# Attention, MLP and capacity routing on one core: the product with v turned round, sums beside it, maxima placed by a mask

## The chip, the cores and the metric

The kernel runs on one core of one Trainium2 chip. The core has a matrix engine (PE, whose weight loads the profile lists apart as PEld), a vector engine (DVE), a scalar engine (ACT), GpSimd (POOL) and a sync engine (SP), whose queue issues nearly all transfers here. Each engine works through its own instructions in order and waits on semaphores. The metric is the device time of one execution in microseconds. In the profile a tile's name is the name given in the code, without buffer numbers.

## The reference

Three stages follow each other: attention with normalised q and k, an MLP with a gated activation, and a mixture of experts with a fixed capacity.

```python
batch, n_heads, seq, head_dim = (4, 12, 448, 64)

def _attn_ref(q, k, v, g_q, g_k):
    def rmsnorm(x, g):
        rms = np.sqrt(np.mean(x * x, axis=-1, keepdims=True) + 1e-06)
        return x / rms * g
    q_n, k_n = (rmsnorm(q, g_q), rmsnorm(k, g_k))
    scale = 1.0 / np.sqrt(q.shape[-1])
    scores = scale * np.matmul(q_n, k_n.transpose(0, 1, 3, 2))
    scores = scores - np.max(scores, axis=-1, keepdims=True)
    attn = np.exp(scores)
    attn = attn / (np.sum(attn, axis=-1, keepdims=True) + 1e-09)
    return np.matmul(attn, v).astype(np.float32)

def _moe_ref(x, w_in, w_out):          # x: 1792 tokens of 768
    h = x @ w_in                       # 768 x 2048
    relu6 = np.clip(h + 3.0, 0.0, 6.0)
    g = h * relu6 / 6.0
    return (g @ w_out).astype(np.float32)
```

The third stage (`_moe2_ref`) gives each of 1792 tokens to one of 8 experts by its logits, at most 224 tokens to each, and runs two products with a ReLU between them per expert. The weights `w_in` and `w_out` arrive as 64-bit floats; everything else is 32-bit.

## The kernel before

The 48 heads are worked on in 24 pairs `i`, six pairs to a batch. The two heads of a pair (`s` = 0, 1) stand in the two halves of the 128 partitions where the contraction runs over the 64 values of a head, and a head's 448 positions are cut into four blocks `c` of 112 (`CP`). Precision is held by splitting: a float32 value becomes a rounded part (`...h`) and a remainder (`...l`) in the type float32r, and a product becomes three.

The steps of a pair, with the names that the profile shows:

- `load` (L208): q, k and v of the pair into `ld_q`, `ld_k`, `ld_v`, 224 KB each.
- `sums`, `invert` (L224, L242): squares on ACT, their sums on DVE, inverse roots on DVE. For the first three pairs the squares read `ld_q` and `ld_k`; for all others, which are done in groups of three or six, q and k are loaded a second time, into `sq` (L237). There are seven groups.
- `norm` (L251): POOL multiplies (`xn`). `transp` (L290): four transposes each for q and k on PE, then ACT writes the rounded part (`qh`, `kh`) and DVE the remainder (`ql`, `kl`).
- `s1` (L313): a first product q k in one rounded part, queries in partitions, from which DVE takes the maxima `mx`. `mt` (L326): PE transposes the maxima, ACT copies them negated (`mrow`), and two small transfers put them as a row into `mr`.
- `sT` (L338): the full scores `st`, keys in partitions, with the row of maxima added by a product with `onerow`; ACT takes the exponentials `ph`.
- `av` (L363): the product with v. The weights (the stationary side) are `va`, 112 keys by 128 columns, 64 of them v and 64 of them ones; the moving side is `ph`, 448 queries wide, in plain float32. So the numerators of a head stand in 64 partitions of `av` and copies of the sums in the other 64.
- `fin`, `fin_r`, `fin_x` (L381 to L415): ACT copies the sums (`sm`) and numerators (`num`), a transfer turns the row of sums into columns (`scol`), DVE takes the reciprocals, a transfer writes them to memory (`r_dr`), another reads them back spread over 64 partitions per head (`rc`), POOL multiplies, ACT writes the rounded part `xh`, POOL the remainder `xl`.

`xh` and `xl` of a batch are the input of the MLP's first product (`h`, L447), 288 products a batch, in the order that `mlp1_atoms` gives. These and, late in the attention, the products that fold the gate's weights into `w_out` (`wprime_atoms`) stand in a list from which `fill` takes some between the steps of later pairs. `conv_in` and `conv_out` narrow the 64-bit weights meanwhile: each of 32 blocks is loaded into the one buffer `wraw`, taken apart by four DVE instructions (`cv`, L128 to L131) and written back.

The order on PE is written out by hand. Each step of a pair has a due time in a table, 16 units to a pair; events are sorted by it, and `fill` spreads the list of atoms between them. For ACT, DVE, POOL and SP the recording layer chooses the order from its own estimate. The table's lines that matter:

```python
T_LOAD, T_NORM, T_Q, T_K, T_V = -56, -38, -30, -29, -5
T_S1, T_MT = (-24, -20, -16, -12), -9.5
T_ST, T_AV, T_FIN = (0, 4, 8, 12), ((4.5, 8.5, 12.5, 14.5), (9, 13, 17, 20)), 2
T_R, T_X, T_MLP = 4, (6, 9, 12), 16
```

PSUM is one pool of eight banks for all of this. After the attention come the last batch's first product, the second product (`y`, L1039), the routing, and the experts.

Of the kernel before, what the change touches and what calls it, by code (L numbers as in the profile page):

```python
# [8 lines left out]
F32 = mybir.dt.float32  # L9
# [4 lines left out]
OP = mybir.AluOpType  # L14
# [7 lines left out]
def kernel(  # L22
# [31 lines left out]
    PB = 4  # L54
# [11 lines left out]
    FULL = B * H  # L66
# [12 lines left out]
    r_dr = [dram.tile([2, S], F32, name=f"r_dr{i}")[:] for i in range(B * NP)]  # L79
# [92 lines left out]
    onerow = const.tile([128, CP], F32R, name="onerow")  # L172
    nc.vector.memset(onerow.bitcast(F32), 0.0)
    eps = const.tile([128, 1], F32, name="eps")
    nc.vector.memset(eps, 1e-9)
    mrs = []
    for s in range(2):
        nc.vector.memset(onerow[64 * s:64 * s + 1, :].bitcast(F32), 1.0)
    for n in range(OB):
        mrs.append(apool.tile([128, S], F32R, name=f"mr{n}", bufs=1))  # L180
        nc.gpsimd.memset(mrs[n].bitcast(F32), 0.0)
    VS = {}

    def vtiles(i):

        f = full(2 * i)
        key = (f, i % 2)
        if key not in VS:
            va = apool.tile([CP, 2, NCH, 128], F32 if f else F32R, name="va", bufs=2)
            w = va if f else va.bitcast(F32)  # L190
            nc.gpsimd.memset(w[:, 0, :, 64:], 1.0)
            nc.gpsimd.memset(w[:, 1, :, :64], 1.0)
            vl = None
            if not f:
                vl = apool.tile([CP, NCH, 192], F32R, name="vl", bufs=2)
                nc.gpsimd.memset(vl[:, :, 64:128].bitcast(F32), 0.0)
            VS[key] = va, vl
        return VS[key]

# [4 lines left out]
    def full(h):  # L204

        return h < FULL

    def load(i):  # L208
        b, j = divmod(i, NP)
        ts = []  # L210
        for nm, src in (("q", q), ("k", k), ("v", v)):
            t = apool.tile([CP, 2, NCH, D], F32, name=f"ld_{nm}")
            nc.sync.dma_start(t.rearrange("p h c d -> p h (c d)"),
                              src[b, 2 * j:2 * j + 2].rearrange("h (p c) d -> p h (c d)", p=CP))
            ts.append(t)
        QKV[i] = ts
# [3 lines left out]
    GROUPS = [(0,), (1,), (2,), (3, 4, 5)] + [tuple(range(g, g + 6)) for g in range(6, NH2, 6)]  # L220
# [1014 lines left out]
```

## Time and profile before

| | us |
|---|---|
| median of 3 runs | 1428.04 |
| lowest, highest run | 1416.88, 1430.52 |
| the profiled execution | 1415.71 |
| its span, first to last instruction | 1413.9 |
| mean granted clock of PE | 0.941 |

In the profile's head each engine's busy time stands with its share of the span:

```profile
span 1413.9 us, 19042 instructions
PE 1219.4 (86%) x6704; PEld 934.2 (66%) x6704; DVE 762.0 (54%) x1517; ACT 589.8 (42%) x1115; POOL 436.9 (31%) x320
PE   1477688878788979977878999999999989999998
PEclk9987889998899999999999999999999999999999
```

The last two lines cut the span into 40 slices of 35 us; a digit is the busy share of PE, and below it the share of its clock that was granted, in tenths. A float32 product is two records on PE, so the 192 products with v are 384 of the 6704. The attention covers the first 754 us, which are the slices in which PE has gaps.

### The profile page before, as it was taken

How to read it: one execution, taken by the hardware profiler on the slowest of the kernel's cores; microseconds unless marked ns; L12 is line 12 of the kernel's file. 1: busy time of each engine (PE TensorE's matmuls, PEld its weight loads, DVE VectorE, ACT ScalarE, POOL GpSimd, SP SyncE). 2: the span in 40 equal slices, each digit the busy share in tenths (PEclk: the TensorE clock that was granted, in tenths of full speed). 3: DMA queues.
4: the chain of work that ended last, by engine and by line, in shares of the span. 5: the costliest groups of instructions: out<-in, count | busy, mean ns of one | idle time of the engine just before them, and what ended most of it. 6: DMA issues, size and time to landing. Idle time of an engine off the chain costs nothing.

```text
span 1413.9 us, 19042 instructions
## 1 busy us (share of the span) xinstructions
PE 1219.4 (86%) x6704; PEld 934.2 (66%) x6704; DVE 762.0 (54%) x1517; ACT 589.8 (42%) x1115; POOL 436.9 (31%) x320
## 2 busy tenths in 40 slices
PE   1477688878788979977878999999999989999998
PEld 1233345555555656655557778777777779999997
DVE  6775655655462323333225974666666657666550
ACT  3354544333344434544445753111111256666650
POOL 1211222212121221211113442222222457767641
PEclk9987889998899999999999999999999999999999
DMA  7776655665663333233238984222222488888741
GB/s 185 206 213 174 163 155 159 192 193 171 182 189 93 93 104 81 80 105 91 79 98 263 321 269 131 60 75 69 63 74 58 113 229 232 248 251 255 228 152 40
DMA packets 247232, 216.97 MB, mean 153 GB/s; under 512 B 32160, under 2 KB 226400, under 8 KB 247136
## 3 DMA queue, kind: packets, MB, share of 16 engines
q1 hardware_dynamic: 243808, 204.74, 50.4%
q0 software_dynamic: 3328, 11.01, 2.5%
q8 instruction: 53, 0.87, 0.3%
q14 instruction: 43, 0.35, 0.1%
HBM read 177.17 MB, written 38.36 MB: 152 GB/s over the span
## 4 chain that ended last, share of the span: by engine, by line
PE 48%; DMA 27%; DVE 12%; issue 5%; ACT 4%; POOL 2%; SPq 1%; POOLq 0%; DVEq 0%; ACTq 0%
PE y L1039 14%; DMA rc<-r_dr 9%; PE h L447 8%; PE y L1187 7%; PE av L370 6%; PE h L1123 4%; DMA r_dr<-rcol 4%; DMA wraw<-in_moe_w_in_dram 3%; DMA wraw<-in_moe_w_out_dram 2%; DMA scol<-sm 2%; PE h L1125 2%; DMA sq<-in_q_dram 2%; PE st L345 2%; DMA win_v<-w 2%; DMA sq<-in_k_dram 2%
## 5 line engine op out<-in xcount | busy, mean ns | idle before, releaser
L370 PE MATMUL av<-ph,va 112*128 112x448 f32 x384 | 200.4, 651 | 33.1 <-DVE kl L307 15.6
L447 PE MATMUL h<-xh,wl 128*128 128x448 f32 x384 | 171.3, 446 | 0.0
L447 PE MATMUL h<-xh,wh 128*128 128x448 f32 x384 | 149.6, 389 | 9.3 <-ACT ph L354 5.9
L370 PEld LDWEIGHTS av<-ph,va 112*128 112x128 f32 x384 | 76.6, 219 | 110.1 <-issue 62.6
L447 PE MATMUL h<-xl,wh 128*128 128x448 f32 x384 | 148.9, 388 | 0.0
L983 POOL TENSOR_TENSOR g2l<-gr,g2h 128x512 fp32r<-128x512 f32 x60 | 78.6, 1311 | 202.0 <-ACT g2h L981 154.7
L106 POOL TENSOR_TENSOR wel<-we_s,weh 128x768 fp32r<-128x768 f32 x60 | 117.8, 1971 | 62.3 <-ACT weh L105 51.5
L105 ACT ACTIVATE weh<-we_s 128x768 fp32r<-128x768 f32 x128 | 105.7, 843 | 71.6 <-DMA we_s<-in_moe_w_dram 53.8
L106 DVE TENSOR_TENSOR wel<-we_s,weh 128x768 fp32r<-128x768 f32 x68 | 99.7, 1473 | 64.0 <-ACT weh L105 58.1
L1039 PE MATMUL y<-woh,g2l 128*128 128x512 f32 (+1 forms) x448 | 128.3, 348 | 1.0 <-POOL g2l L983 1.0
L322 DVE TENSOR_REDUCE mx<-s 112x1 f32<-112x448 f32 x192 | 110.4, 613 | 33.1 <-PE s L319 33.1
L1039 PE MATMUL y<-woh,g2h 128*128 128x512 f32 (+1 forms) x448 | 127.1, 347 | 0.0
L1039 PE MATMUL y<-wol,g2h 128*128 128x512 f32 (+1 forms) x448 | 126.0, 345 | 0.0
L981 ACT ACTIVATE g2h<-gr 128x512 fp32r<-128x512 f32 x60 | 37.7, 631 | 205.6 <-PE y L1039 157.5
L1123 PE MATMUL h<-xe,weh 128*128 128x448 f32 x384 | 121.2, 378 | 2.6 <-DVE xe L1074 2.6
L411 POOL TENSOR_TENSOR num<-num,rc 128x448 f32<-128x448 f32 x24 | 27.2, 1131 | 298.9 <-DMA rc<-r_dr 287.2
L354 ACT ACTIVATE ph<-st 112x448 f32<-112x448 f32 x192 | 93.0, 538 | 50.8 <-PE st L345 50.0
L106 POOL TENSOR_TENSOR wl<-win_v,wh 128x768 fp32r<-128x768 f32 x32 | 61.6, 1925 | 154.4 <-ACT wh L105 133.8
L447 PEld LDWEIGHTS h<-xh,wh 128*128 128x128 f32 x384 | 76.7, 200 | 29.5 <-issue 12.3
L447 PEld LDWEIGHTS h<-xh,wl 128*128 128x128 f32 x384 | 76.5, 199 | 25.2 <-issue 17.4
L1125 PE MATMUL h<-xe,wel 128*128 128x224 f32 x384 | 92.8, 269 | 0.0
L1187 PE MATMUL y<-weh,hl 128*112 128x384 f32 x256 | 86.5, 338 | 0.0
(235 smaller groups left out, 2496.2 us busy)
## 6 DMA issues: line engine op xcount, KB each, us to landing
we_s<-in_moe_w_dram SPq DMA_DIRECT2D x128, 384.0 KB
win_v<-w SPq DMA_DIRECT2D x64, 384.0 KB
g_dr<-g SPq DMA_DIRECT2D x64, 224.0 KB
gr<-g_dr SPq DMA_DIRECT2D x52, 256.0 KB
wraw<-in_moe_w_in_dram SPq DMA_DIRECT2D x16, 768.0 KB
wraw<-in_moe_w_out_dram SPq DMA_DIRECT2D x16, 768.0 KB
gr<-g_dr SPq DMA_DIRECT2D x48, 224.0 KB
w<-cv SPq DMA_DIRECT2D x16, 384.0 KB
```

What stands on the lines that cost most here:

```text
L105: nc.scalar.activation(hi, raw, AF.Copy)
L106: eng.tensor_tensor(lo, raw, hi.bitcast(F32), op=OP.subtract)
L322: mx = nc.vector.tensor_reduce(MX[i][:, s * NCH + c:s * NCH + c + 1], pp[s][:CP, :S], axis=AX.X, op=OP.max)
L354: nc.scalar.activation(e[:, s], pp[s][:CP, :S], AF.Exp)
L370: nc.tensor.matmul(p[:, :S], va[:, s, c, :], a, start=(c == 0), stop=(c == NCH - 1))
L447: nc.tensor.matmul(p[:, :S], w[:, c], x[:, c], start=(n == 0), stop=(n == 3 * NC - 1))
L981: nc.scalar.activation(gh, g, AF.Copy)
L983: eng.tensor_tensor(gl, g, gh.bitcast(F32), op=OP.subtract)
L1039: nc.tensor.matmul(pp[hf][:, :COLS[hf].stop - COLS[hf].start], a[:, f % QF], w[:, COLS[hf]], start=(f == 0 and n == 0), stop=(f == NF - 1 ...
L1123: mm = [lambda: nc.tensor.matmul(p[:, :4 * CP], wh[:, fo], x.rearrange("d k t -> d (k t)"), start=(c == 0), stop=(c == NC - 1), skip_group ...
L1125: lambda: nc.tensor.matmul(p[:, :2 * CP], wl[:, fo], x[:, 0], start=False, stop=False, skip_group_check=True)]
L1187: nc.tensor.matmul(p[:CP, :HW], a[:, f, tk], w[:, o], start=(f == 0 and n == 0), stop=(f == FB - 1 and n == 2))
```

## The change

The product with v changes sides. The exponentials, 112 keys by 112 queries, become the stationary side, and v with two columns of ones (66 columns, `vv`) the moving side. The queries then stand in the partitions, the numerators and the sums beside each other in one row. DVE adds 1e-9 to the sums (`scol`), copies the numerators (`num`), takes the reciprocals, POOL multiplies with them along the row (`xq`), PE turns the result back by four transposes (`xt`), ACT writes `xh` and DVE `xl`, both from PSUM. The transfers `scol`, `r_dr` and `rc` are gone.

The maxima are transposed as before, from a tile with a column for each block at 0 to 3 and 64 to 67, and DVE multiplies the result, repeated four times, with a mask (`place`) that keeps row `c` in block `c`; a product with -1 everywhere (`minus`) then sums over the partitions. `mrow` and its transfers are gone.

q and k are loaded once, each into three buffers; v is loaded by a step of its own, later. The squares are taken from these loads, in groups of one, one, and then two pairs (13 groups), through one buffer `sq` instead of two.

The due times are new. The product with v of a pair stands after all its scores, beside those of the next pair, one head after the other; the number of `ph` buffers goes from 4 (two heads each) to 12 (one head each).

The ACT queue in the second stage, where an MLP product runs beside the pairs, before the change:

```order
L354 ACTIVATE ph<-st 112x448 x2
L390 ACTIVATE sm<-av,eps 1x448
L392 ACTIVATE num<-av 64x448
L283 ACTIVATE va<-ld_v 112x4x64
L390 ACTIVATE sm<-av,eps 1x448
L392 ACTIVATE num<-av 64x448
L283 ACTIVATE va<-ld_v 112x4x64
L354 ACTIVATE ph<-st 112x448 x2
L105 ACTIVATE wh<-win_v 128x768
```

and a few rows on in the same pair:

```order
L354 ACTIVATE ph<-st 112x448 x2
L413 ACTIVATE xh<-num 128x448
L330 ACTIVATE mrow<-t 8x112
L105 ACTIVATE wh<-win_v 128x768
L450 ACTIVATE r<-h,half 128x448
L354 ACTIVATE ph<-st 112x448 x4
```

The same engine and place after the change:

```order
L319 ACTIVATE ph<-st 112x448 x2
L252 ACTIVATE vv_113<-ld_v 112x8x64
L107 ACTIVATE wh<-win_v 128x768
L417 ACTIVATE r<-h,half 128x448
L319 ACTIVATE ph<-st 112x448 x2
L381 ACTIVATE xh<-t 128x448
L107 ACTIVATE wh<-win_v 128x768
L417 ACTIVATE r<-h,half 128x448
L319 ACTIVATE ph<-st 112x448 x2
```

The copies of sums and numerators and the row of maxima have left ACT, and `xh` now reads PE's transposes (`t`) instead of POOL's `num`.

The DVE queue in the second stage after the change, where a block of `w_out` is converted (`cv`) beside a pair; `mr` are the placed maxima, and `scol` and `num` read the product with v:

```order
L130 TENSOR_SCALAR cv<-wraw 128x768
L419 SCALAR_TENSOR_TENSOR g<-r,h 128x448
L289 TENSOR_REDUCE mx_109<-s_1721 112x1
L289 TENSOR_REDUCE mx_109<-s_1722 112x1
L131 TENSOR_SCALAR cv<-cv 128x768
L297 TENSOR_TENSOR mr<-t,place 128x448
L363 TENSOR_SCALAR scol<-av,eps 112x4
L364 COPY num<-av 112x4x64
L132 SCALAR_TENSOR_TENSOR cv<-wraw,cv 128x768
L368 RECIPROCAL scol<-scol 112x8
```

Of these rows `mr`, `scol` and `num` are new on DVE, and they stand behind the first `cv`, which waits for a transfer.

The SP queue at the start of the program, the loads of the first pairs, before the change (`sq` is the second load of q and k):

```order
L213 DMA ld_q<-in_q_dram 112x2x256
L213 DMA ld_k<-in_k_dram 112x2x256
L213 DMA ld_v<-in_v_dram 112x2x256
L237 DMA sq<-in_q_dram 112x2x256
L237 DMA sq<-in_k_dram 112x2x256
L213 DMA ld_v<-in_v_dram 112x2x256
L556 DMA wg<-in_moe_w_gate_dram 128x6x8
L213 DMA ld_q<-in_q_dram 112x2x256
L213 DMA ld_k<-in_k_dram 112x2x256
```

and after it:

```order
L200 DMA ld_q<-in_q_dram 112x2x256
L200 DMA ld_k<-in_k_dram 112x2x256
L200 DMA ld_q<-in_q_dram 112x2x256
L200 DMA ld_k<-in_k_dram 112x2x256
L207 DMA ld_v<-in_v_dram 112x2x256 x2
L523 DMA wg<-in_moe_w_gate_dram 128x6x8
L207 DMA ld_v<-in_v_dram 112x2x256
L200 DMA ld_q<-in_q_dram 112x2x256
L200 DMA ld_k<-in_k_dram 112x2x256
```

Both pieces begin with the second pair's q and k; the third pair's stood seven rows on and now stand next.

The diff, cut to its core:

```diff
-    PB = 4
+    PB = 12
+    SQ = 1
+    SPLIT = False
-    T_LOAD, T_NORM, T_Q, T_K, T_V = -56, -38, -30, -29, -5
-    T_S1, T_MT = (-24, -20, -16, -12), -9.5
-    T_ST, T_AV, T_FIN = (0, 4, 8, 12), ((4.5, 8.5, 12.5, 14.5), (9, 13, 17, 20)), 2
-    T_R, T_X, T_MLP = 4, (6, 9, 12), 16
+    T_LOAD, T_VLOAD, T_NORM, T_Q, T_K, T_V = -72, -20, -38, -30, -28, 6
+    T_SUMS, T_INV = -50, -42
+    T_S1, T_MT = (-24, -20, -16, -12), -7
+    T_ST = (0, 4, 8, 12)
+    T_AV = ((17, 18, 19.5, 20.5), (22, 23, 24.5, 25.5))
+    T_NUM, T_XT, T_MLP = 28, 31, 35
...
+    place = const.tile([128, NCH, CP], F32, name="place")
+    nc.vector.tensor_tensor(place, ident[:, 0:NCH, None].to_broadcast([128, NCH, CP]),
+                            ident[:, 64:64 + NCH, None].to_broadcast([128, NCH, CP]), op=OP.add)
...
-    GROUPS = [(0,), (1,), (2,), (3, 4, 5)] + [tuple(range(g, g + 6)) for g in range(6, NH2, 6)]
+    GROUPS = [(0,), (1,)] + [(g, g + 1) for g in range(2, NH2, 2)]
...
-        for a, src in ((0, q), (1, k)):
-            sq = apool.tile([CP, 2 * NCH, D], F32, name="sq", bufs=2)
-            if len(g) == 1:
-                x = QKV[i][a]
-            else:
-                x = sq.rearrange("p (h c) d -> p h c d", h=2)
-                nc.sync.dma_start(x.rearrange("p h c d -> p h (c d)"),
-                                  src[b, 2 * j:2 * j + 2].rearrange("h (p c) d -> p h (c d)", p=CP))
-            nc.scalar.activation(sq, x.rearrange("p h c d -> p (h c) d"), AF.Square)
+        for a in range(2):
+            sq = apool.tile([CP, 2 * NCH, D], F32, name="sq", bufs=SQ)
+            nc.scalar.activation(sq, QKV[i][a].rearrange("p h c d -> p (h c) d"), AF.Square)
...
-        nc.tensor.transpose(t[:2 * NCH, :CP], MX[i], ident[:CP, :CP])
-        m = apool.tile([2 * NCH, CP], F32R, name="mrow")
-        nc.scalar.activation(m, t[:2 * NCH, :CP], AF.Copy, scale=-1.0)
-        MR[i] = mrs[i % OB]
-        for s in range(2):
-            nc.sync.dma_start(MR[i][64 * s:64 * s + 1].rearrange("a (c p) -> a c p", c=NCH).bitcast(F32),
-                              m[s * NCH:(s + 1) * NCH].bitcast(F32))
+        nc.tensor.transpose(t[:, :CP], MX[i].rearrange("p h c -> p (h c)"), ident[:CP, :CP])
+        MR[i] = apool.tile([128, NCH, CP], F32R, name="mr")
+        nc.vector.tensor_tensor(MR[i], t[:, None, :CP].to_broadcast([128, NCH, CP]), place, op=OP.mult)
...
-                nc.tensor.matmul(p[:, :S], va[:, s, c, :], a, start=(c == 0), stop=(c == NCH - 1))
+                nc.tensor.matmul(p[:CP, o:o + W], PP[i, s, c][0][:, qs], vv[:, s, c, 64:], start=(c == 0), stop=(c == NCH - 1))
...
+            nc.vector.tensor_scalar(sc[:, s, m], pv[:, :, 64], eps[:CP], None, op0=OP.add)
+            nc.vector.tensor_copy(num[:, m, s], pv[:, :, 0:64])
+
+    def normalize(i):
+        num, sc, xq = NUM[i]
+        nc.vector.reciprocal(sc, sc)
+        nc.gpsimd.tensor_tensor(xq, num, sc[:, :, :, None].rearrange("p h c o -> p c h o").to_broadcast([CP, NCH, 2, D]),
+                                op=OP.mult)
+
+    def xt(i):
...
+        for c in range(NCH):
+            nc.tensor.transpose(t[:, c * CP:(c + 1) * CP], xq[:, c].rearrange("p h d -> p (h d)"), ident[:CP, :CP])
+        nc.scalar.activation(xh[:, j], t[:, :S], AF.Copy)
+        nc.vector.tensor_tensor(xl[:, j], t[:, :S], xh[:, j].bitcast(F32), op=OP.subtract)
```

In the new `av` the loop runs over heads, blocks of queries `n` (`qs`) and blocks of keys `c`; `W` is 66, and four blocks of queries share one PSUM bank.

More of the change, by code (lines that the diff above doesn't have):

```diff
@@ L174 @@
     eps = const.tile([128, 1], F32, name="eps")
     nc.vector.memset(eps, 1e-9)
-    mrs = []
-    for s in range(2):
[L178 to L198, printed above, removed]
+    mxs = []
@@ L201 @@
+    for n in range(2):
+        mxs.append(apool.tile([CP, 2, 64], F32, name=f"mx{n}", bufs=1))
+        nc.gpsimd.memset(mxs[n], 0.0)
+    VW = 130
+    vvs = []
+    for n in range(2):
+        vvs.append(apool.tile([CP, 2, NCH, VW], F32R if SPLIT else F32, name=f"vv{n}", bufs=1))
+        nc.gpsimd.memset((vvs[n].bitcast(F32) if SPLIT else vvs[n])[:, :, :, 128:], 1.0)
     QKV, OPER, XT, FIRST, TR = {}, {}, {}, {}, {}
     NH2 = B * H // 2
-    def full(h):
-        return h < FULL
     def load(i):
@@ L395, in fin_r @@
-    def fin_r(i):
-        sc, num = SM[i]
-        rs = apool.tile([CP, 2, NCH], F32, name="rcol", bufs=2)
-        nc.vector.reciprocal(rs, sc)
-        nc.sync.dma_start(bass.AP(tensor=r_dr[i].tensor, offset=r_dr[i].offset, ap=[[NCH, CP], [S, 2], [1, NCH]]), rs)
-        rc = apool.tile([128, S], F32, name="rc", bufs=2)
-        nc.sync.dma_start(rc, bass.AP(tensor=r_dr[i].tensor, offset=r_dr[i].offset, ap=[[S, 2], [0, 64], [1, S]]))
-        SM[i] = (rc, num)
-    def fin_x(i, part):
+        for s in range(2):
+            if SPLIT:
+                e = apool.tile([CP, S], F32, name="pexp", bufs=2)
+                ph, pl = [apool.tile([CP, S], F32R, name=n, bufs=PB) for n in ("ph", "pl")]
+                nc.scalar.activation(e, pp[s][:CP, :S], AF.Exp)
+                nc.scalar.activation(ph, e, AF.Copy)
+                nc.gpsimd.tensor_tensor(pl, e, ph.bitcast(F32), op=OP.subtract)
+                PP[i, s, c] = (ph, pl)
+            else:
+                e = apool.tile([CP, S], F32, name="ph", bufs=PB)
+                nc.scalar.activation(e, pp[s][:CP, :S], AF.Exp)
+                PP[i, s, c] = (e,)
@@ L405, in fin_x @@
+    def normalize(i):
[4 more added lines that the diff above has]
+    def xt(i):
         b, j = divmod(i, NP)
-        rc, num = SM[i]
-        if i % NP == 0 and part == 0:
+        xq = NUM.pop(i)[2]
+        if j == 0:
             XT[b] = [xpools[b % 2].tile([128, NC, S], F32R, name=n) for n in ("xh", "xl")]
@@ L409, in fin_x @@
         xh, xl = XT[b]
-        if part == 0:
-            nc.gpsimd.tensor_tensor(num, num, rc, op=OP.mult)
-        elif part == 1:
-            nc.scalar.activation(xh[:, j], num, AF.Copy)
-        else:
-            nc.gpsimd.tensor_tensor(xl[:, j], num, xh[:, j].bitcast(F32), op=OP.subtract)
+        t = ps.tile([128, 512], F32, name="t", tag="b", bufs=8)
+        for c in range(NCH):
+            nc.tensor.transpose(t[:, c * CP:(c + 1) * CP], xq[:, c].rearrange("p h d -> p (h d)"), ident[:CP, :CP])
@@ L653 @@
         at(t + T_LOAD, load, i)
[L654 to L661 removed]
+        at(t + T_VLOAD, vload, i)
+        g = GROUP[i]
+        first = 16 * g[0]
+        at(first + T_SUMS + 4 * (i - g[0]), sums, i)
+        if i == g[-1]:
+            at(first + T_INV, invert, g)
+        at(t + T_NORM, norm, i)
         at(t + T_Q, transp, i, 0)
```

153 lines of the change are left out of this document (60 added, 93 removed).

## The prediction

> **What bounds the kernel now.** I read the busy time by stage first. The attention runs to 754 us: six pairs of heads without MLP work, then twelve with the MLP's first product of an earlier batch between them, then the last five, into which the work on the gate's weights is merged.
>
> ```profile
> 0.00:209.00 209.00, 127.17 (x494) 66.17 (x494) 135.46 (x273) 91.76 (x180) 40.84 (x44) 0.86 0.69 181
> 209.00:567.00 358.00, 302.72 (x1359) 203.14 (x1358) 160.23 (x262) 148.22 (x285) 85.14 (x66) 0.91 0.50 146
> 567.00:754.00 187.00, 151.67 (x787) 107.77 (x787) 57.45 (x118) 82.37 (x181) 30.87 (x24) 0.92 0.34 98
> 754.00:1413.00 659.00, 637.84 (x4072) 557.08 (x4070) 408.84 (x864) 267.42 (x471) 280.01 (x188) 0.99 0.56 165
> ```
>
> The columns are the stretch, its length, then PE, weight loads, DVE, ACT, POOL, the granted clock, the DMA share and GB/s. After 754 us PE is busy 638 of 659 us at clock 0.99, and no edit lies there: I carry that stretch over. Before it PE is idle for 754 - 582 = 172 us, and its busy time ran at 0.86, 0.91 and 0.92 of its clock, which lost 127 x 0.14 + 303 x 0.09 + 152 x 0.08 = 57 us. No other engine is full. So next come the waits of PE before 750 us.
>
> ```profile
> PE t L295 <- POOL xn L263: 27.6, 2, 14.0
> PE s L319 <- ACT mrow L330: 26.9, 8, 5.1
> PE t L328 <- DVE mx L322: 24.7, 10, 4.9
> PE av L370 <- DVE kl L307: 15.6, 4, 7.4
> PE av L370 <- ACT ph L354: 12.9, 5, 6.2
> PE lg L590 <- ACT ph L354: 7.9, 1, 7.9
> PE st L345 <- ACT num L392: 7.6, 5, 2.3
> PE st L345 <- ACT ph L354: 7.3, 4, 4.6
> PE s L319 <- DVE mx L322: 6.3, 4, 2.6
> PE h L447 <- ACT ph L354: 5.9, 2, 5.8
> PE s L319 <- ACT ph L354: 4.6, 1, 4.6
> PE h L447 <- ACT mrow L330: 3.2, 2, 2.8
> ```
>
> Each row gives who waited for whom, the total, how often, and the longest. ACT ends 26.9 + 12.9 + 7.9 + 7.6 + 7.3 + 5.9 + 4.6 + 3.2 = 76 us of these waits, although it is under half busy. The waits of ACT and POOL, and the chain of waits of one pair, say why.
>
> ```profile
> ACT xh L413 <- POOL num L411: 149.1, 19, 13.6
> POOL num L411 <- DMA rc<-r_dr: 287.2, 23, 32.3
> 302.85 3.81 DMA scol<-sm
> 306.75 0.21 DVE rcol L398
> 306.98 5.92 DMA r_dr<-rcol
> 312.93 8.06 DMA rc<-r_dr
> 321.12 1.17 POOL num L411
> ```
>
> The sums of a pair go through three transfers that follow each other (3.8 + 5.9 + 8.1 us), then POOL multiplies, then ACT copies (xh). ACT works in order: while xh waits, the exponentials (ph) and the row of maxima (mrow) behind it wait too, and PE waits for those. So a latency of some 18 us a pair holds up queues whose engines have time to spare.
>
> **The change, part by part.** The sums are made against the profiled run, 1415.7 us (span 1413.9). The three runs shown have their median at 1428.0, 0.9% higher, and their lowest at 1416.9.
>
> *The three transfers go.* The sums now stand beside the numerators in PSUM, so a pair needs two DVE reads, a reciprocal, one POOL multiply, four transposes on PE and the ACT copy. ACT's copy waits for PE and no longer for a transfer, and it stands some 1.5 pairs behind the exponentials that it belongs to. Of the 76 us I take three quarters as gone, -57; what is late next in the rest is ACT's own work and DVE. The wait for kl (15.6) is a wait for DVE, which waited for ACT's kh in its turn at least once (8.6 of it in the row below); I take half, -8. Ends: 0 and -92.
>
> ```profile
> DVE kl L307 <- ACT kh L304: 8.6, 1, 8.6
> sq<-in_q_dram SPq DMA_DIRECT2D x21, 224.0 KB
> ```
>
> *q and k are loaded once.* 21 transfers of 224 KB for q (the row above) and as many for k go, and on SP's queue the loads of the third pair's q and k now stand ahead of everything that waits. The two long PE waits for xn (27.6) belong to the second and third pair, whose loads stood behind v and the second loads: half, -14 (ends 0 and -28). The new price is that the squares read ld_q and ld_k through one buffer: ACT's square of k waits for DVE's sum of q. I put it at nothing, because two exponentials stand between the two squares on ACT; if DVE is late, that cover is gone, and the case is in the rivals.
>
> *The product with v.* Before, a pair took 16 records of 448 columns; now it takes 64 of 66 columns (32 float32 products, two records each), with the exponentials as weights, 112 columns to load for each record. What bounds such a record is shown by these rows of PE and of its weight loads:
>
> ```profile
> 325.01 1.77 PE L370 MATMUL av<-ph,va 112*128 112x448 f32 x4
> 326.81 0.36 PE L447 MATMUL h<-xh,wh 128*128 128x448 f32 x1
> 325.49 0.19 PEld L370 LDWEIGHTS av<-ph,va 112*128 112x128 f32 x1 [0.19 <-issue]
> 325.87 0.19 PEld L370 LDWEIGHTS av<-ph,va 112*128 112x128 f32 x1 [0.19 <-issue]
> 1260.20 0.27 PE L1125 MATMUL h<-xe,wel 128*128 128x224 f32 x1
> 1260.31 0.37 PE L1123 MATMUL h<-xe,weh 128*128 128x448 f32 x1
> 1260.21 0.19 PEld L1123 LDWEIGHTS h<-xe,weh 128*128 128x128 f32 x1
> 1249.90 1.31 PE L1071 MATMUL xp<-ident,xr 112*128 112x112 f32 x12
> ```
>
> A float32 record of 448 columns takes 0.38 us: the loads of two that follow each other start at 325.49 and 325.87, and they run while a product is under way, on the same 112 rows. So 16 records are 6.0 us, and by columns one of 66 would take 0.38 x 66 / 448 = 0.055. The load is longer: where a product of 224 columns is followed by another weight tile, that load starts with the product (1260.21 against 1260.20) and the next product starts 0.11 later, about when 128 columns are in; 112 columns are then 0.095. The twelve transposes give the same, (1.31 - 0.26) / 11 = 0.095 with 0.26 for the last one's length. 64 x 0.095 = 6.1 us a pair: turning the product round changes PE by +0.1 x 24 = +2 us. The ends are 64 x 0.055 = 3.5 (loads fully hidden) and 64 x 0.15 = 9.6 (load and product one after the other): -60 and +86 us. I take 0.095, from the row in which a load really bounds.
>
> The Trainium skill ("TensorE: Matmul & The Clock Gate", Part 3, "What overlaps and what doesn't") says that a weight load overlaps with products in flight only where the row groups differ. By that rule the +86 us end would hold, and the time would be that of the third rival below, 1433. The rows at 325 us speak against it here: those loads use the same rows as the products beside them and cost nothing.
>
> *The result is turned back* by four transposes a pair: 24 x 4 x 0.095 = +9 us on PE, which is full in the second stage; ends 0 and +18.
>
> *Work moves to DVE.* POOL and ACT get less, DVE more:
>
> ```profile
> L1032 DVE COPY ysb<-y 128x256 f32<-128x256 f32 x14 | 5.9, 422 | 6.8 <-PE y L1039 6.8
> L852 DVE TENSOR_TENSOR G<-rt,cap 40x8 bf16<-40x8 f32 x42 | 6.6, 158 | 42.4 <-PE rt L850 42.4
> L1074 DVE TENSOR_TENSOR xe<-xp,xe 128x448 fp32r<-128x448 f32 x24 | 13.6, 615 | 12.1 <-ACT xe L1073 11.9
> L247 DVE SCALAR_TENSOR_TENSOR st<-st 112x96 f32<-112x96 f32 x9 | 3.0, 333 | 0.1
> DVE cv L128 <- DMA wraw<-in_moe_w_out_dram: 51.9, 15, 6.9
> DVE cv L128 <- DMA wraw<-in_moe_w_in_dram: 39.3, 14, 9.5
> ```
>
> Per pair: placing the maxima by the mask 0.62 (as the xe row, from PSUM, 448 wide), xl likewise 0.62, two copies of 112x256 at 0.42, two additions of 112x4 at 0.16: 2.4 us, 58 in all. The inverse roots are taken in 13 groups where there were 7: 6 x 11 instructions on shorter rows than in the fourth line, under 0.33 each; I take 0.25, some 16 us. DVE's 135 + 160 + 57 = 353 us before 754 become 427. PE waited for DVE's mx 24.7 + 6.3 = 31 us, 0.09 us per us of DVE's work; 74 more are 7, and since the placed maxima and the reads of PSUM now stand in that queue I double it: +14. Ends 0 and +74. The row of maxima no longer makes its own two transfers; its wait (mrow) is counted above.
>
> *Clock.* With fewer idle stretches PE's clock is higher. The waits fall from 172 us to about 172 - 57 - 8 - 14 + 14 = 107, more than a third; of the 57 us lost I take a third back, -19 (ends 0 and -35).
>
> **Sum:** -57 - 8 - 14 + 2 + 9 + 14 - 19 = -73, so 1415.7 - 73 = 1343. The runs shown lie up to 1% above the profiled one, so for the time of a run I put half the distance of their median on it: 1349.
>
> **Rivals.** *DVE becomes the bound.* All of the 74 us lands on PE's way instead of 14: 1349 + 60 = 1409. For it: DVE is busy 135 of 209 us in the first stage, and eight pairs of 2.4 bring it to 155 there. Against it: in the other two it is under half busy.
>
> *The slow one: the new work waits behind the weights' conversion.* DVE stands still 91 us (51.9 + 39.3, 29 times, 9.5 at the longest) until a raw weight block has landed, and now the placed maxima, the reads of the product and the reciprocal are queued behind such waits, with PE's transposes of xq behind them in order. Between a pair's last product and these transposes lie 5.5 of a pair's 16 steps, 9 us at some 27 us a pair (358 / 12 = 30 before); the reads, the reciprocal, the multiply and the rest of one conversion need about 5 of them. A wait over 4 us there stops PE. If all 91 and all 74 land on PE, the time is 1349 - 14 + 91 + 74 = 1500; slower than before begins where 0.6 of it does. I put this case at 1455. Against it: the same waits cost PE 31 us until now, and 42 transfers less should shorten them.
>
> *Load and product don't overlap* (the upper end above): 1349 - 2 + 86 = 1433, if PE bounds everywhere; in the first stage it does not, so this is its worst. Against it stand the rows at 325 us. *The transfers were covered anyway*, and ACT is late because PE's products reach it late: it waited 50 us for st in its own row below, against 149 for POOL. Then the terms -57, -8 and -19 don't come: 1349 + 84 = 1433.
>
> ```profile
> ACT ph L354 <- PE st L345: 50.0, 34, 5.9
> ```
>
> **Chances.** The forecast 0.64, DVE as the bound 0.14, the slow one 0.13, no overlap 0.04, covered transfers 0.05. About 1% either way can't be told from no change with this kernel. Faster by over 1%: 0.64 and 0.09 of the DVE case, 0.73. Slower by over 1%: 0.13 and 0.03 of the last two, 0.16. Within 1%: 0.11. The range: its lower end takes the better ends of the waits (-92 - 28 - 35 instead of -57 - 8 - 14 - 19, 57 lower) and a part of the product's (-17): 1275. Its upper end takes in the DVE case and the near half of the other three: 1425. The forecast's own range is 1275 to 1400.
>
> **What would show it.** ACT's wait for POOL's multiply (149 us) is gone and nothing of 100 us stands in its place; PE's waits for ACT before the attention's end are under 30 us; the product's records start 0.09 to 0.10 us apart (0.15: no overlap; 0.06: loads free); the clock of the middle stage is 0.94 or more; DVE is busy some 425 us in the attention; PE's wait for xn is 14 us or less. The attention then ends near 685 us. It is wrong if PE waits for DVE's mr, num or mx, or for xq, by more than 70 us, if DVE's waits for wraw grow, or if the stretch after the attention changes its length.

## The result, and the profile after

| | before | after |
|---|---|---|
| median, us | 1423.66 (4 runs) | 1378.59 (4 runs) |
| lowest to highest | 1416.88 to 1430.52 | 1376.34 to 1385.91 |
| ratio, 95% interval | | 0.971, 0.967 to 0.975 |
| span of the profiled execution | 1413.9 | 1377.8 |

The change makes the kernel 2.9% faster, 45 us. That is inside the range, but 30 us short of the forecast. The head of the page after the change:

```profile
span 1377.8 us, 21118 instructions
PE 1242.1 (90%) x7952; PEld 1052.3 (76%) x7952; DVE 819.4 (59%) x1726; ACT 527.7 (38%) x971; POOL 406.6 (30%) x293
PE   2676766699999999999999999999999889999997
PEclk9655555779999999999999999999999999999999
```

A slice is 34 us here. From the tenth slice on PE is busy at nearly its full clock, and the next slices under 0.9 come only after the attention (slices 32, 33 and 40). But in slices 3 to 7 only half of its clock was granted, where before it was 0.7 to 0.9. So the gain has to be read in two stages. The ninth pair's scores (`st`) divide them, since from there the MLP's products stand between all pairs in both kernels; they start at 242.57 us before and at 297.50 after. The windows of before, with the columns of the first table of the prediction:

```profile
0.00:243.00 243.00, 155.06 (x609) 84.20 (x611) 150.71 (x298) 105.54 (x208) 49.25 (x50) 0.87 0.67 180
243.00:754.00 511.00, 426.49 (x2029) 292.88 (x2026) 202.43 (x356) 216.81 (x438) 107.61 (x83) 0.91 0.44 127
```

And of after:

```profile
0.00:297.00 297.00, 191.29 (x938) 149.96 (x939) 188.20 (x382) 72.82 (x137) 39.30 (x40) 0.63 0.50 149
297.00:715.00 418.00, 413.57 (x2943) 347.10 (x2942) 224.29 (x480) 187.84 (x364) 88.06 (x67) 0.99 0.39 116
376.00:559.00 183.00, 183.00 (x1319) 154.32 (x1318) 102.45 (x227) 84.70 (x152) 44.17 (x35) 1.00 0.34 101
715.00:1377.00 662.00, 637.25 (x4074) 555.27 (x4074) 406.88 (x864) 267.04 (x471) 279.20 (x188) 0.99 0.55 165
```

The part behind the first stage lost 93 us (511 to 418). In the middle of it, from 376 to 559 us, PE has no idle time at all at full clock: eight pairs at 22.9 us each. The first stage grew by 54 us (243 to 297). The stretch after the attention is 662 us long instead of 659.

Each stage can be taken apart with these rows: idle time is length minus PE's busy time, clock loss is busy time times the missing share of the clock (an average, so good to a few us), and the rest is work at full clock.

| us | idle | clock loss | work |
|---|---|---|---|
| first stage before | 88 | 155 x 0.13 = 20 | 135 |
| first stage after | 106 | 191 x 0.37 = 71 | 120 |
| rest of the attention before | 85 | 426 x 0.09 = 38 | 388 |
| rest of the attention after | 4 | 414 x 0.01 = 4 | 409 |
| sum before | 173 | 58 | 523 |
| sum after | 110 | 75 | 529 |

The split between idle time and clock loss holds for the one execution that was profiled, and it should not be read as a cause. The clock records of these traces show only two values, 0.5 and 1.0, so a mean clock gives the time at half clock: twice the missing share of the span. The four executions after the change had mean clocks of 0.914 (the profiled one), 0.917, 0.931 and 0.966, which is an estimated 237, 228, 190 and 94 us at half clock. They took 1379.5, 1376.3, 1377.7 and 1385.9 us. The one with 143 us less at half clock was not faster; it was the slowest. So in this kernel a higher clock does not by itself shorten the time, and something other than PE must set the pace of the first stage, where nearly all the half clock of the profiled execution lies.

PE's waits before 750 us, after the change:

```profile
PE t L380 <- POOL xq L369: 47.5, 7, 10.5
PE s L286 <- ACT kh L272: 15.8, 5, 5.2
PE t L263 <- POOL xn L246: 13.2, 2, 7.7
PE t L263 <- DVE xn L246: 11.1, 1, 11.1
PE s L286 <- ACT ph L319: 6.5, 4, 2.3
PE av L348 <- DVE ql L275: 3.2, 1, 3.2
PE st L308 <- ACT ph L319: 3.2, 2, 2.3
PE s L286 <- DVE mx L289: 3.0, 4, 1.4
```

ACT ends 15.8 + 6.5 + 3.2 = 26 us of them, where it was 76. What is new is `xq`, 47.5 us in seven waits, all in the first stage: PE's transposes of the finished heads wait for POOL's multiply, which waits for DVE. What holds DVE and SP there is seen in their queues. SP's waits in the first 300 us, after:

```profile
SPq L147 <- DVE cv L133: 79.6, 10, 9.4
SPq L157 <- DVE cv L133: 68.3, 9, 9.4
```

and the same kind of rows before:

```profile
SPq L145 <- DVE cv L131: 15.8, 7, 6.4
SPq L155 <- DVE cv L131: 6.8, 3, 4.8
```

SP stands 148 us in front of the write-backs of narrowed weight blocks (`w_in` and `w_out`), where the same two rows made 23 us before. What this does to the pairs is seen on SP's queue around 140 us:

```profile
135.62 0.54 SPq L140 DMA_DIRECT2D wraw<-in_moe_w_in_dram  x1
136.21 0.89 SPq L200 DMA_DIRECT2D ld_q<-in_q_dram  x1
146.19 0.37 SPq L147 DMA_DIRECT2D w<-cv  x1
146.66 0.49 SPq L200 DMA_DIRECT2D ld_k<-in_k_dram  x1
```

The load of k of one pair goes out 10 us after the load of q of the same pair, since the write-back between them waits for DVE, and DVE waits for the raw block that SP issued just before. ACT then waits for these loads, and for PE's late transposes:

```profile
ACT sq L225 <- DMA ld_q<-in_q_dram: 88.2, 20, 11.4
ACT xh L381 <- PE t L380: 68.8, 19, 10.9
ACT sq L225 <- DMA ld_k<-in_k_dram: 44.7, 14, 8.1
```

The due times of the conversions are not in the diff. But the order of SP, DVE, ACT and POOL is chosen by the recording layer from its own estimate, and in the changed kernel it pulled the conversions ahead: before the ninth pair's scores 27 blocks of weights were loaded, 17 before the change. The 32 raw blocks go out one after the other, from 16.7 to 338.1 us, so one every 10.4 us; 27 of them are an estimated 281 us, nearly the whole first stage.

### The profile page after: what moved, and what is told of

The parts are those of the page before. It is cut to its first block, busy times and chain, and to the rows that moved or that the text cites. A ratio compares the mean times of both kernels' runs of the same rounds, so it can differ in the third digit from the quotient of the medians.

```text
span 1377.8 us, 21118 instructions
## 1 busy us (share of the span) xinstructions
PE 1242.1 (90%) x7952; PEld 1052.3 (76%) x7952; DVE 819.4 (59%) x1726; ACT 527.7 (38%) x971; POOL 406.6 (30%) x293
## 4 chain that ended last, share of the span: by engine, by line
PE 60%; DVE 16%; DMA 16%; issue 5%; SPq 1%; ACT 1%; POOL 1%; POOLq 0%; DVEq 0%; ACTq 0%
PE h L414 14%; PE y L1002 14%; PE y L1150 7%; PE av L348 7%; DMA wraw<-in_moe_w_in_dram 6%; DMA wraw<-in_moe_w_out_dram 5%; PE h L1086 4%; PE st L308 4%; PE h L1088 2%; DVE cv L133 2%; DVE cv L132 2%; PE rt L813 1%; DVE mx L289 1%; DVE cv L130 1%; DVE cv L131 1%
## 5 line engine op out<-in xcount | busy, mean ns | idle before, releaser
L348 PEld LDWEIGHTS av<-vv,ph 112*112 112x112 f32 x1536 | 203.9, 208 | 20.8 <-issue 12.3
L348 PE MATMUL av<-vv,ph 112*112 112x66 f32 x1536 | 207.9, 290 | 3.2 <-DVE ql L275 3.2
L414 PE MATMUL h<-xh,wh 128*128 128x448 f32 x384 | 156.3, 407 | 0.1
L414 PE MATMUL h<-xh,wl 128*128 128x448 f32 x384 | 144.7, 377 | 0.8 <-POOL wl L108 0.8
L414 PE MATMUL h<-xl,wh 128*128 128x448 f32 x384 | 144.1, 375 | 0.0
L108 DVE TENSOR_TENSOR wel<-we_s,weh 128x768 fp32r<-128x768 f32 x68 | 96.0, 1419 | 71.0 <-ACT weh L107 60.8
L369 POOL TENSOR_TENSOR xq<-num,scol 112x512 f32<-112x512 f32 x24 | 26.6, 1110 | 258.7 <-DVE scol L368 220.0
L1150 PE MATMUL y<-weh,hh 128*112 128x384 f32 x256 | 86.3, 337 | 0.0
L1150 PE MATMUL y<-wel,hh 128*112 128x384 f32 x256 | 86.3, 337 | 0.0
```

The lines of the kernel that those rows point to most:

```text
L108: eng.tensor_tensor(lo, raw, hi.bitcast(F32), op=OP.subtract)
L348: nc.tensor.matmul(p[:CP, o:o + W], PP[i, s, c][0][:, qs], vv[:, s, c, 64:], start=(c == 0), stop=(c == NCH - 1))
L414: nc.tensor.matmul(p[:, :S], w[:, c], x[:, c], start=(n == 0), stop=(n == 3 * NC - 1))
L1150: nc.tensor.matmul(p[:CP, :HW], a[:, f, tk], w[:, o], start=(f == 0 and n == 0), stop=(f == FB - 1 and n == 2))
```

## Experiments

The runs were made on several chips, each beside the kernel before, so ratios to the kernel before are compared.

| run | median, us | ratio (95%) |
|---|---|---|
| after | 1378.59 | 0.971 (0.967 to 0.975) |
| second loads of q, k put back | 1393.19 | 0.980 (0.975 to 0.984) |
| row of maxima put back | 1380.13 | 0.970 (0.968 to 0.972) |
| both put back, only the turned product left | 1391.28 | 0.977 (0.976 to 0.979) |
| conversions paced | 1321.05 | 0.928 (0.924 to 0.933) |
| before, conversions paced | 1438.93 | 1.012 (1.010 to 1.014) |
| 128 columns | 1332.83 | 0.937 (0.933 to 0.941) |
| 96 columns | 1326.30 | 0.932 (0.930 to 0.933) |
| 80 columns | 1382.34 | 0.972 (0.968 to 0.976) |
| 66 columns in the order of 96 | 1361.71 | 0.955 (0.949 to 0.961) |
| paced, 128 columns | 1303.81 | 0.914 (0.908 to 0.921) |
| paced, 96 columns | 1292.80 | 0.910 (0.905 to 0.916) |
| paced, 96 columns, later turn | 1296.95 | 0.911 (0.906 to 0.916) |

### Which part of the change pays

The second loads of q and k put back, with the seven groups, and two buffers for each of q and k instead of three:

```diff
-    GROUPS = [(0,), (1,)] + [(g, g + 1) for g in range(2, NH2, 2)]
+    GROUPS = [(0,), (1,), (2,), (3, 4, 5)] + [tuple(range(g, g + 6)) for g in range(6, NH2, 6)]
...
+                nc.sync.dma_start(x.rearrange("p h c d -> p h (c d)"),
+                                  src[b, 2 * j:2 * j + 2].rearrange("h (p c) d -> p h (c d)", p=CP))
```

> The squares again read second loads of q and k, in the groups and at the due times of the kernel before; the turned product and the mask stay. Theory squares: ACT's waits for the loads of q and k fall by half and the first stage gets shorter by 20 us or more, time 1360 or less. Theory conversions: 42 transfers more on the same queue make no gain; the ninth pair's scores start at 290 us or later and the time is 1375 to 1400.

It takes back 15 us, and the ninth pair's scores start at 312 us, as the second theory had it. In this run PE's wait for POOL's `xn` is 28.9 us, against 13.2 after, so about what was booked for it (14) did come from here. DVE's waits for `wraw` stay as long (102 us against 100).

The row of maxima put back in place of the mask:

```diff
-        MR[i] = apool.tile([128, NCH, CP], F32R, name="mr")
-        nc.vector.tensor_tensor(MR[i], t[:, None, :CP].to_broadcast([128, NCH, CP]), place, op=OP.mult)
+        nc.scalar.activation(m, t[:2 * NCH, :CP], AF.Copy, scale=-1.0)
+        MR[i] = mrs[i % OB]
+        for s in range(2):
+            nc.sync.dma_start(MR[i][64 * s:64 * s + 1].rearrange("a (c p) -> a c p", c=NCH).bitcast(F32),
+                              m[s * NCH:(s + 1) * NCH].bitcast(F32))
```

> The changed kernel with the row of maxima made as before: ACT copies it (mrow), two small transfers put it into mr, three units earlier than in the changed kernel. Theory transfers (the mask takes a latency off ACT's and SP's way): PE waits again for mrow or mr, 10 to 30 us in all, time 1385 to 1405. Rival (the mask only moves work onto DVE, whose conversions set the pace of the first stage): DVE has 15 us less to do, the first stage gets shorter by some 10 us, time 1362 to 1376.

> Only the turned product is left of the change: second loads of q and k for the squares (as in e4, which took 15 us more than the changed kernel) and the row of maxima by transfers (as in e5). If the parts are independent, the time is 1379 + 15 + what e5 shows, 1390 to 1420. If the turned product alone carries the gain, it is 1385 to 1397; if the gain needs the cleared queue of SP, it is over 1415, no better than before.

The mask is worth nothing that can be measured in this order of queues (1380 against 1379; the intervals lie in each other), and the time lies between the ranges of both theories. It could hardly show: with the transposes of the maxima 2.5 steps earlier PE waits 44 us for DVE's `mx`, where all such rows make 6 us after, and even that costs nothing; its wait for `xq` is 12 us shorter instead. With both put back 32 us remain of the 45: the product turned round brings most of the gain by itself, and loading q and k once some 11 to 15. The expectations for both put back overlap, and 1391 lies in the first two. All three runs keep the first stage's fault: their clock between 90 and 232 us is 0.54, 0.52 and 0.52, as it is 0.52 after, and in each 27 blocks are loaded before the ninth pair's scores. So neither the 42 loads nor the small transfers of the maxima made the room that the conversions took. The three transfers of the sums and the new due times are among the reasons left; they were not tested apart.

### The conversions pulled ahead

Each raw block's load now waits for the last score product that was written down before it, so it can't be moved ahead of its place; the blocks of `w_in` get even due times:

```diff
+    def hold(ld):
+        tc.add_manual_dep(ld.ins, MX.get("last", MX["first"]).ins.name,
...
+        hold(nc.sync.dma_start(raw.rearrange("p f t -> p (f t)"), w_out.bitcast(I32)[rows, :]))
...
-        at(8 * (CI0 + CI1 * u if u < CI else H + 1 + CI2 * (u - CI)), conv_in, u)
+        at(14 + 11 * u, conv_in, u)
```

> Each load of a raw weight block waits for the last score product that stands before it in the program, and the blocks of w_in are spread over 11 steps each, so conversions can no longer be pulled ahead of their place. Theory conversions: the ninth pair's scores start before 255 us instead of 297, DVE's conversions go on to about 480 us, the middle stage keeps 23 us a pair, and the time falls by 30 us or more, to 1350 or less. Theory clock: the clock stays at 0.5 to 0.6 in the first stage and the time falls by 15 us at most. Theory squares (the loads of q and k are waited for by ACT's squares): ACT's wait for ld_q and ld_k, 96 us before 300 us, stays above 60 and the time falls by less than 15 us.

It gains 57 us over after, and the theory of the conversions holds, though they go on to 607 us and not to 480. (The wait and the even due times were not tested apart.) DVE's waits for `wraw`, first after the change, then with the pacing, fall to half:

```profile
DVE cv L130 <- DMA wraw<-in_moe_w_in_dram: 51.0, 14, 6.2
DVE cv L130 <- DMA wraw<-in_moe_w_out_dram: 49.1, 16, 4.9
```

```profile
DVE cv L130 <- DMA wraw<-in_moe_w_out_dram: 25.1, 12, 3.8
DVE cv L130 <- DMA wraw<-in_moe_w_in_dram: 23.0, 8, 7.2
```

and the ninth pair's scores start at 225 us instead of 297, with 10 blocks loaded before them. The same edit on the kernel before:

> The kernel before, with its conversions held to their place and spread as in e2. Theory new cost (conversions ran ahead so far only in the changed kernel, 27 blocks before the ninth pair's scores against 17 before): the time stays within 1% of 1420. Rival (conversions held up the kernel before in the same way): 1370 to 1400, a gain of the size that e2 showed over the changed kernel.

There it costs 1.2%, a little more than the 1% of the first theory, and the rival is out. PE's longest waits in that run:

```profile
PE s L321 <- ACT mrow L332: 43.5, 9, 6.8
PE av L372 <- ACT ph L356: 35.9, 9, 8.7
```

So the conversions' place was no fault of the kernel before, where PE's longest waits are for ACT. It became one with the change.

### The width of the product's records

After the change a record of the product with v moves 66 columns while the next 112 columns of weights are loaded. By the row of the prediction (0.38 us for 448 columns) the columns move for 0.055 of a record's 0.095 us. To see whether that lowers the clock, the moving side is made wider in the first seven pairs; the columns added are ones that are not read.

```diff
-        W = VW if SPLIT else 66
+        W = 128 if i < 7 else 66
+        lo = VW - W
...
-                nc.tensor.matmul(p[:CP, o:o + W], PP[i, s, c][0][:, qs], vv[:, s, c, 64:], start=(c == 0), stop=(c == NCH - 1))
+                nc.tensor.matmul(p[:CP, o:o + W], PP[i, s, c][0][:, qs], vv[:, s, c, lo:], start=(c == 0), stop=(c == NCH - 1))
```

> For the first seven pairs the product with v runs with 128 moving columns instead of 66 (62 of them carry ones and are not read), so that a record's product lasts longer than its weight load. Theory clock (in the first stage PE stays at half clock because products that are bound by their weight loads do not count as enough activity): the granted clock between 90 and 232 us rises from 0.50 to 0.60 to over 0.8 and the time falls by 15 to 30 us, to 1350 to 1365 us. Theory conversions (the first stage runs at the pace of the weight blocks that are loaded, converted and stored one after the other, ahead of their place): the clock may rise, but PE only waits longer; the time stays within 6 us of 1378.

> As e1_wide, with 96 moving columns instead of 128 for the first seven pairs: a record's product is then 0.080 us at full clock, still shorter than the load of 0.095. If the clock follows the share of time in which columns move (0.58 for 66 columns, 0.84 for 96, 1 for 128), the granted clock between 90 and 232 us lies between that of the changed kernel (0.5 to 0.6) and 0.82, and the time between 1333 and 1379. If only a product longer than its load lifts the clock, it stays at 0.6 or less and the time above 1370.

> After with 80 moving columns in the first seven pairs; 14 columns of ones are unread. Columns move in 0.38 x 80 / 448 = 0.068 of a record's 0.095 us, a share of 0.71 between 0.58 (1378.6 us, 229 us at half clock) and 0.84 (1326.3 us, 106 us). Theory: the granted clock follows the share bit by bit: 1345 to 1360 us, about 165 us at half clock. Rivals: there is a step between 0.71 and 0.84, and nothing changes: 1374 to 1383; or a step between 0.58 and 0.71, and the whole gain is there already: 1322 to 1333.

(The time at half clock in these expectations is the sum of the stretches before 720 us in which the trace's clock records show 0.5: 229 us after, 92 with 128 columns, 106 with 96, 188 with 80.) With 128 and 96 columns the time falls by 46 and 52 us, more than any of their theories had, though PE moves more columns; the clock lies where the theories of the clock had it. With 80 the time doesn't fall at all, as the first rival had it, although the time at half clock does. The rows of the stretch from 90 to 232 us, first of after, then with 96 columns, then with 80:

```profile
90.00:232.00 142.00, 94.87 (x470) 76.95 (x470) 82.22 (x156) 28.65 (x57) 14.28 (x12) 0.52 0.46 137
```

```profile
90.00:232.00 142.00, 103.72 (x671) 83.10 (x670) 98.75 (x199) 44.00 (x84) 20.35 (x17) 0.78 0.50 143
```

```profile
90.00:232.00 142.00, 86.47 (x479) 68.91 (x476) 81.31 (x158) 29.77 (x58) 13.80 (x12) 0.62 0.47 142
```

The last row is the telling one. With 80 columns the clock is higher than after (0.62), PE is busy for less time, and it gets through about the same number of records (479 against 470). The ninth pair's scores start at 297.50 us in both, and a raw block goes out every 10.4 us in both. The clock was raised and the time didn't follow, just as in the execution after the change with a mean clock of 0.966; so in this order something else ends last: the chain of raw blocks. The queues show that the recording layer had answered to the width as well. Ahead of the ninth pair's placed maxima DVE's queue holds the work on 26 blocks of weights with 66 columns and on 27 with 80, but only on 18 with 96. The two runs with 128 and 96 columns had changed two things.

### Order and width apart

The columns stay at 66, and the raw blocks' loads are kept behind the same loads of q, k and v as in the run with 96 columns, by a rule of order on SP's queue that adds no wait:

```diff
+    K_AT = [0, 0, 0, 0, 1, 3, 3, 5, 7, 10, 12, 14, 16, 18, 21, 24, 26, 29, 32]
+    V_AT = [0, 0, 0, 0, 6, 7, 10, 13, 14, 17, 19, 22, 25, 27, 30, 32]
...
+            i = max(j for j, m in enumerate(a) if m <= n)
...
+                tc.add_manual_dep(ld.ins, LD[nm, i].ins.name,
+                                  mybir.DependencyInfo(mybir.DependencyClass.NoSync, mybir.DependencyReason.DATA),
```

> After with its 66 columns, and the loads of the raw weight blocks kept behind the same loads of q, k and v as the queue of the run with 96 columns has them. The recording layer had changed that order with the width: ahead of the placed maxima of the ninth pair DVE's queue holds the work on 26 blocks of weights with 66 columns and on 27 with 80, but on 18 with 96, and on 19 here. So 96 against 66 columns changed two things. Theory A, the share of moving columns alone: the order is worth nothing, 1370 to 1385 us, and the clock between 90 and 232 us stays near 0.52. Theory B, the order alone: the time of the run with 96 columns, 1322 to 1335 us. Theory C, both: with the paced order 96 columns were worth 28 us (1321.1 to 1292.8), so the order is the rest, 1326 + 28 = 1354, 1346 to 1362 us, clock 0.60 to 0.70.

Theory C holds, at the upper edge of its numbers: 1361.7 us, and 0.60 of the clock:

```profile
90.00:232.00 142.00, 99.40 (x564) 80.93 (x564) 79.80 (x158) 35.34 (x68) 17.14 (x15) 0.60 0.44 128
```

So of what 96 columns bring, the order is 17 us (23 by the ratios) and the width 35 (33 by the ratios). DVE's queue is not the same to the row in these two runs (19 blocks against 18), so the split is good to some us.

### Both remedies, and the best version

> Both edits. If conversions and clock each hold a part, the time is below both alone, 1320 to 1340 us, with a clock over 0.8 in the first stage. If the clock is only a consequence of the waits, it is the time of the paced kernel alone within 4 us; if conversions are no cause, it is that of the wide one alone.

> The third run (paced weight blocks and 128 moving columns) with 96 columns in the first seven pairs instead; 30 columns of ones are unread. Theory: the two losses of the first stage are separate, so 96 columns are worth here what they were without the pacing (1326.3 against 1332.8): 1294 to 1300 us, clock 0.96. Rival: with the weight blocks paced PE is no longer the limit of the first stage, and the shorter records only lengthen its waits: 1302 to 1307 us.

Both edits gain more than was expected: 1304 us with 128 columns, under the 1320 to 1340, and 1293 with 96, just under the 1294 to 1300. With the blocks paced, SP's order of raw blocks and loads is the same with 66 and with 96 columns, so this is the cleanest test of the width: 1321 us with 66, 1293 with 96, and the intervals of the ratios lie apart (0.924 to 0.933, 0.905 to 0.916). The rows with 66, then with 96:

```profile
90.00:232.00 142.00, 114.19 (x682) 94.19 (x681) 83.65 (x175) 43.14 (x83) 23.42 (x19) 0.69 0.39 116
```

```profile
90.00:232.00 142.00, 117.41 (x833) 97.34 (x832) 94.35 (x193) 52.07 (x98) 26.86 (x22) 0.86 0.46 134
```

In this order the clock counts: in four executions with 96 columns the mean clock and the time go together, 0.958 with 1301.5 us, 0.966 and 0.967 with 1290.9 and 1294.7, 0.970 with 1287.0. Whether 96 are better than 128 here can't be told; their intervals overlap. The run with 96 columns is the best version, 9.0% under before and some 6% under after. Its two stages:

```profile
0.00:202.00 202.00, 141.59 (x938) 112.85 (x939) 140.64 (x313) 73.31 (x137) 37.63 (x40) 0.83 0.43 122
202.00:626.00 424.00, 412.93 (x2944) 345.38 (x2944) 278.38 (x549) 187.81 (x365) 96.93 (x68) 1.00 0.52 160
```

The ninth pair's scores start at 202 us. PE gets through the same 938 records up to there as after, in 95 us less: 45 less idle (106 to 60) and 50 less busy, nearly all of it clock (0.63 to 0.83). The second row has nearly the length that it has after (424 against 418): both remedies act in the first stage.

What PE still waits for longest there is `xq`, 29.7 us. The last run puts its transposes 4 of a pair's 16 steps later:

```diff
-    T_NUM, T_XT, T_MLP = 28, 31, 35
+    T_NUM, T_XT, T_MLP = 28, 35, 39
```

> As the run before it, and the transposes of xq stand 4 of a pair's 16 steps later on PE (the MLP's product of the batch too). PE waited 21 us for xq in the first 300 us of the paced 128-column run. Theory: POOL's multiply is then done in time, the wait falls below 8 us, and 10 to 16 us of the time go: 1281 to 1290 us. Rival: the wait is only moved, to the keys' and queries' roundings (kh, ql) that stand behind the same engines: within 4 us of the run before it.

The wait is gone from PE's seven longest rows in the first 300 us, and the ninth pair's scores start at 175 us, 27 us earlier. Yet the time is the same within the intervals (1297 against 1293), and the attention's last `xl` ends at 629.5 us against 625.5. Neither theory was right: the rival has about the size, but PE's wait for `kh` is 8.2 us against 8.0, and the wait was not moved there. PE's windows say where the lead went, with 96 columns paced:

```profile
200.00:300.00 100.00, 94.67 (x660) 78.66 (x659) 67.17 (x125) 42.40 (x78) 23.56 (x17) 0.98 0.57 165
300.00:400.00 100.00, 97.05 (x689) 81.11 (x688) 75.44 (x157) 45.64 (x84) 27.29 (x19) 1.00 0.56 176
```

and with the later turn:

```profile
200.00:300.00 100.00, 91.48 (x588) 75.35 (x587) 63.89 (x124) 39.49 (x70) 22.32 (x17) 0.93 0.51 154
300.00:400.00 100.00, 97.89 (x660) 82.03 (x660) 69.54 (x142) 42.15 (x76) 23.01 (x17) 0.94 0.50 161
```

PE is busy about as long but at 0.93 and 0.94 of its clock, and does 101 records fewer in these 200 us. With the later turn, pairs with 1 to 5 us of idle time on PE take 26 to 33 us up to 490 us, the others 23 to 25. The lead was given back later, in short gaps and in lower clock; which edit would hold it was not tried.

## Why the prediction was right, and where it was not

**The mechanism was right.** The latency of the three transfers went, and with it most of PE's waits for ACT: 26 us are left of 76, forecast under 30 (a row of 3.3 us for `kh`, which the prediction's list leaves out, would make it 79). The term was -57 and is -50. The wait for `kl` went from 15.6 to `ql`'s 3.2 (-12, forecast -8), POOL's `xn` from 27.6 to 13.2 (-14, as forecast). DVE's `mx` did not grow; of 31 us some 6 are left (3.0 in the row shown), where +14 were booked. That room was taken by `xq`, 47.5 us, for which the sum had no term of its own. In all PE's idle time before the attention's end went from 173 to 110 us; the sum had 172 to 107. That this total agrees is partly luck: `mx` and `xq` missed by some 40 us and more in opposite directions, and nearly all that is left stands in the first stage, where idle time even grew (88 to 106).

**The product costs what was forecast.** Eight of its records, and the weight loads beside them, in the middle of the attention:

```profile
403.80 0.91 PE L348 MATMUL av<-vv,ph 112*112 112x66 f32 x8
403.80 0.77 PEld L348 LDWEIGHTS av<-vv,ph 112*112 112x112 f32 x7
```

With 0.26 for the last one's length as in the prediction, (0.91 - 0.26) / 7 = 0.093 us from record to record, forecast 0.095. Work at full clock in the attention is 529 us against 523, forecast +11. The rival in which load and product don't overlap is out, and with it, for these products, the rule of the Trainium skill ("TensorE: Matmul & The Clock Gate", Part 3, "What overlaps and what doesn't") that a weight load overlaps only where row groups differ: seven loads of 0.19 us on the rows of the running products fit into 0.77 us beside them.

**The clock term had the wrong sign, and behind it the pace of the first stage was missing.** The step read: "With fewer idle stretches PE's clock is higher", -19. It is right behind the first stage, where the clock loss fell from 38 to 4 us and the middle stage has a clock of 1.00 (forecast 0.94 or more). In the first stage of the profiled execution it rose from 20 to 71. Together that is +17 instead of -19, 36 us, and the attention ends at 715 us instead of 685. As bookkeeping this is the whole error. As a cause it is not: the execution with a mean clock of 0.966 took 1385.9 us, and 80 columns raised the clock without moving the ninth pair's scores. What the sum lacked is a term for the raw blocks, which hold the first stage at 297 us: with them paced, and the product unchanged, the time fell by 57 us. With the blocks held back PE's clock counts too. The step took it to follow the gaps; with the same order of SP's blocks and loads, 96 columns instead of 66 raise it from 0.69 to 0.86 in the stretch from 90 to 232 us and save 28 us, so it also follows what PE does while it is busy.

**The slow rival came true in part, and one of the prediction's own signs of being wrong came.** That sign was that DVE's waits for `wraw` grow: they went from 91 to 100 us. PE's wait for `xq` (47.5 us) stayed under the 70 that were named, and the stretch after the attention changed by 3 us (659 to 662). The rival had the right place. The argument against it, "42 transfers less should shorten them", was the wrong inference: with these 42 put back the waits are 102 us. The prediction did not reckon with the recording layer, which placed the conversions ahead of the loads that the pairs need; which part of the change led it to is not shown. The price, from the pacing, is up to 57 us; part of that goes with the clock, which pacing alone raises from 0.52 to 0.69. Order and clock overlap: each remedy alone brings 46 to 57 us, both together 75 to 86.

**DVE as the bound** did not come: it is busy 412 us up to 715, forecast some 425, and in the second stage PE hardly waits for it. Loading q and k once was worth what was booked (11 to 15 against 14). Its price, put at nothing, shows as 133 us in which ACT's squares wait for `ld_q` and `ld_k`; but the second loads put back cost time, so these waits did not hold up the stage by themselves. The mask, booked with nothing but its share of DVE's work, gains nothing in this order.

## What to carry to other kernels

When something else chooses the order of an in-order queue, look after each edit at what has moved up in that queue before you price the edit; a wait on a nearby product that pins the filler work, with even due times for it, took a few lines here and was worth more than the edit itself (57 us against 45). When a product is turned so that it becomes shorter than its own weight load, its price in PE time can be right and the clock still be lower; look at the granted clock of the stretch, and then ask whether PE sets the pace there at all: two executions with different clocks and the same time say that it doesn't. And when a test changes a shape, compare the queues of the two kernels before crediting the shape: with 96 columns a third or more of the gain was a changed order.

## What the runs showed of the hardware

In the profiled execution the granted clock stayed at 0.5 from 48 to 208 us after the change, although PE worked without idle time from 127 to 142 us within it. From its rows there, and in the last line the same product as in the first, later and at full clock:

```profile
127.05 0.71 PE L308 MATMUL st<-qh,kh 64*112 64x448 f32 x2
...
129.19 3.25 PE L348 MATMUL av<-vv,ph 112*112 112x66 f32 x16
132.23 0.95 PE L263 MATMUL t<-ident,xn 112*128 112x112 f32 x4
132.98 1.63 PE L348 MATMUL av<-vv,ph 112*112 112x66 f32 x8
...
137.48 4.61 PE L348 MATMUL av<-vv,ph 112*112 112x66 f32 x24
...
375.75 0.46 PE L308 MATMUL st<-qh,kh 64*112 64x448 f32 x2
```

The Trainium skill ("TensorE: Matmul & The Clock Gate", Part 1, "What's actually happening") gives some 3.4 us of sustained work as enough for the full clock. That does not hold here: 15 us of back-to-back records, more than half of that time with short moving sides, were not enough, and the records' lengths bear the clock out (0.71 us against 0.46). Nor is the clock the same in each execution of this kernel: the means of the four go from 0.914 to 0.966. A record of 96 columns takes about as long at half clock as one of 66 (8 in 1.81 us against 8 in 1.63 above):

```profile
117.18 1.81 PE L349 MATMUL av<-vv,ph 112*112 112x96 f32 x8
```

so the wider product fills the same time with more moving columns. That this is what raises the clock was not shown; what exactly the clock counts was not settled. The share of a record in which columns move (0.58, 0.71 and 0.84 by the estimate above for 66, 80 and 96) orders the clocks of that stretch, 0.52, 0.62 and 0.78, but the run with 96 columns had another order of queues too; with that order 66 columns have 0.60.
